# Pooling v ahead of the gather, contiguous exponentials, one second-layer job and products of zeros in a pooled-attention and mixture-of-depths kernel

## The chip, the cores and the metric

The kernel runs on one core of one Trainium2 chip. The metric is the device time of one execution in microseconds (us). Before the change its median is 304.64 us over three runs (303.97 to 305.81). The profile that is read below is of one further execution, whose span from the first to the last instruction is 305.4 us.

The core has five engines that matter here. TensorE (PE) multiplies matrices and writes to PSUM, VectorE (DVE) and ScalarE (ACT) do elementwise work, GpSimd (POOL) does elementwise work on data in SBUF and starts the indirect transfers, and SyncE (SP) starts the loads. PSUM is used here as four single banks (`bank0` to `bank3`) and two accumulators (`pA`).

## The reference

Two blocks follow each other. Attention takes q, k and v of shape (8 batches, 8 heads, 576 tokens, 64); k and v are averaged over windows of 8 tokens, so that 72 pooled keys remain. Then, for each batch, a gate picks 128 of the 576 rows, and these rows go through a two-layer network.

```python
k_p = k.reshape(B, H, Sp, pool, D).mean(axis=3)
v_p = v.reshape(B, H, Sp, pool, D).mean(axis=3)
scores = scale * np.matmul(q, k_p.transpose(0, 1, 3, 2))
attn = softmax(scores)                                # written out in the reference
x = np.matmul(attn, v_p)                              # then (B, H, S, D) -> (B, S, H*D = 512)

scores = np.einsum('bsd,d->bs', x, w_gate)
out = x.copy()
for b in range(B):
    top_idx = np.argpartition(-scores[b], capacity)[:capacity]      # capacity 128
    xe = x[b, top_idx]
    h = np.maximum(xe @ w1, 0.0)                      # w1: 512 x 1024
    ye = h @ w2                                       # w2: 1024 x 512
    g = 1.0 / (1.0 + np.exp(-scores[b, top_idx]))
    out[b, top_idx] = x[b, top_idx] + g[:, None] * ye
```

All inputs and outputs are float32.

## The kernel before

The order of the instructions is written by hand. The work is cut into 21 steps. A step computes the scores of some tokens against the pooled keys (`scores`), their exponentials, the products with the pooled v (`attend`) and the division by the sums (`norm`). Batches go in pairs: a pair (e, o) of an even and an odd batch takes five steps, two of e, one with the last tokens of both, two of o; the first pair takes six (steps 0 to 5), so that step 6 is the first of batch 2. The main loop is this; `run(u, slot)` runs the jobs that were put down for a slot of a step with `at(u, slot, ...)`:

```python
for u in range(NU + 1):
    for a, x in enumerate(chunks):
        if x[0] == u:
            attend(a)
            norm(a)
    run(u, 0)
    if u + 1 < NU:
        scores(u + 1)
    if u < NU:
        store_x(u)
    if u + 2 < NU:
        q_trans(u + 2)
    for slot in range(1, 5):
        run(u, slot)
```

Each engine works through its own instructions in this order. The jobs are: `pool_k` and `pool_v`, which sum the windows of 8 (the last of `pool_v` also multiplies by the gate's weights); `k_trans` and `gate_v` on VectorE, which finish them; `row_bcast`, `count` and `one_hot`, which rank the rows of a batch; `gather`, which fetches the picked rows; `gate`; `x_trans`, which turns them; `hidden`, a half of the first layer; `finish`, a half of the second.

```python
    def pool_v(b, g, eng):
        x = VR[b, g]
        VP[b] = vps[b % 2]
        h = slice(HG * g, HG * g + HG)
        eng.tensor_tensor(out=x[:, :, 0:4, :], in0=x[:, :, 0:4, :], in1=x[:, :, 4:8, :], op=OP.add)
        eng.tensor_tensor(out=x[:, :, 0:2, :], in0=x[:, :, 0:2, :], in1=x[:, :, 2:4, :], op=OP.add)
        eng.tensor_tensor(out=VP[b][:, h, 0:D], in0=x[:, :, 0, :], in1=x[:, :, 1, :], op=OP.add)
        nc.gpsimd.tensor_tensor(out=x[:, :, 2, :], in0=VP[b][:, h, 0:D], in1=wg[:, h, :], op=OP.mult)
    def gate_v(b, g):
        h = slice(HG * g, HG * g + HG)
        nc.vector.tensor_reduce(out=VP[b][:, h, D + 1], in_=VR[b, g][:, :, 2, :], axis=AX.X, op=OP.add)
# ... in scores(), for a step of one batch: 8 exponentials out of four banks, two of each bank
            ET[u] = [[work.tile([128, 2, C], FT, name=f"et{i}{c}") for i in range(4)] for c in range(2)]
            for c in range(2):
                for i in range(4):
                    x = p[i].rearrange("p s one (n t c g) -> p (s one n) c g t", n=2, c=2, g=G)[:, :, c]
                    y = ET[u][c][i].rearrange("p s (n g t) -> p (s n) g t", n=2, g=G)
                    if c == 0:
                        x, y = (z.rearrange("p a g t -> p a t g") for z in (x, y))
                    nc.scalar.activation(y, x, AF.Exp, scale=exp_scale)
# ... in attend(): one product for each head and half, which reads VP[b], the pooled v with its gate's column
                nc.tensor.matmul(PA[a][TL * t : TL * t + TL, g, E * n : E * n + E], e, VP[b][:, h, :], start=True, stop=True)
# ...
        p = accumulator()[:, 0, 0 : 2 * NC].rearrange("p (k c) -> p k c", k=2)
# ... (products with ones, then two operations on VectorE)
    def x_trans(b):
        p = bank([128, DB, cap])
        for d in range(DB):
            nc.tensor.transpose(p[:, d, :], XR[b][:, 128 * d : 128 * d + 128], ident[:cap, :cap])
        XG[b] = work.tile([128, DB, cap], FT, name="xg", bufs=1)
        nc.scalar.copy(out=XG[b], in_=p)
# ...
    def finish(b, part, p):
        idx, g = GV[b]
        if part == 0:
            gate_end(b)
        c = slice(DM // 2 * part, DM // 2 * part + DM // 2)
        p = p.rearrange("p a b -> p (a b)")[:cap, 0 : DM // 2]
        for f in range(FB):
            n, m = divmod(f, FB // 2)
            nc.tensor.matmul(p, HT[b, n][:, m, :], w2[:, f, c], start=(f == 0), stop=(f == FB - 1))
        nc.vector.scalar_tensor_tensor(Y[b][:, c], p, g, XR[b][:, c], op0=OP.mult, op1=OP.add)
        if part == 1:
            i = nc.gpsimd.indirect_dma_start(
                out=out_rows, out_offset=bass.IndirectOffsetOnAxis(ap=idx[:, :1], axis=0), in_=Y[b], in_offset=None)
            others(i, b, (store, scat, gath))
            scat[b] = [i]
    def dense(b, i, first=False):
        p = accumulator()[:, 0, 0 : FB // 2 * cap].rearrange("p (a b) -> p a b", b=cap) if first else bank([128, FB // 2, cap])
        (hidden, finish)[i // 2](b, i % 2, p)
```

The jobs of the first pair and of a later pair (e, o) that isn't the last, cut to what the change touches; `s` is the first step of the pair, and x and y are the two batches of the pair after:

```python
    for b, (steps_of, dense_of) in {
        0: (((2, 1), (3, 0), (3, 3), (5, 0)), ((5, 3, False), (5, 3, False), (6, 1, True), (7, 1, True))),
        1: (((5, 1), (6, 0), (6, 3), (7, 3)), ((8, 1, True), (9, 1, True), (9, 2, False), (10, 1, True))),
    }.items():
        for f, x in zip((row_bcast, one_hot, gather, x_trans), steps_of):
            at(*x, f, b)
        at(*steps_of[0], count, b)
        at(*steps_of[3], gate, b)
        for i, (u, slot, first) in enumerate(dense_of):
            at(u, slot, dense, b, i, first)
# ... for e in range(2, B, 2): s = 6 + 5 * (e // 2 - 1); o = e + 1
            at(s + 5, 3, gather, o)
            at(s + 6, 3, x_trans, o)
            at(s + 6, 3, gate, o)
            for i in range(4):
                at(s + 5 + i // 2, 1 + i % 2, dense, e, i, i % 2 == 0)
            at(s + 7, 2, dense, o, 0)
            at(s + 8, 1, dense, o, 1, True)
            at(s + 8, 2, dense, o, 2)
            at(s + 9, 2, dense, o, 3)
# ...
            at(s + 2, 4, pool_k, x, pool)
            at(s + 2, 4, pool_v, x, 0, pool)
            at(s + 3, 4, pool_v, x, 1, pool)
            at(s + 3, 4, k_trans, x)
            at(s + 4, 4, gate_v, x, 0)
            at(s + 4, 4, gate_v, x, 1)
            at(s + 4, 4, pool_k, y, pool)
            at(s + 5, 4, pool_v, y, 0, pool)
            at(s + 5, 4, k_trans, y)
            at(s + 6, 4, pool_v, y, 1, pool)
            at(s + 6, 4, gate_v, y, 0)
            at(s + 6, 4, gate_v, y, 1)
```

## Time and profile before

| What | Value |
|---|---|
| time, median of three runs | 304.64 us |
| span of the profiled execution | 305.4 us |
| PE matmul busy | 232.1 us (76%), 2922 instructions |
| PE weight load busy | 205.4 us (67%) |
| DVE busy | 139.3 us (46%) |
| POOL busy | 130.7 us (43%) |
| ACT busy | 76.9 us (25%) |
| mean granted TensorE clock | 0.903 |
| moved by DMA | 46.94 MB, mean 154 GB/s |

An engine's busy time is summed over its instructions, and "idle before" a line is the time that the engine stood still ahead of it, with the instruction that released it. Matmuls in float32 show as two records each. L-numbers are lines of the kernel: L323 is the scores, L338 the exponentials, L352 attend, L489 the first layer, L502 and L503 the second, L248 to L252 the pooling of v, L256 `gate_v`, L455 and L457 the gather's index and its start, L479 and L481 `x_trans`, L505 the scatter of the finished rows.

### The profile page before, as it was taken

The page shows a single profiled execution, that of the slowest core. Times are in us where ns is not written, and L with a number is a line of the kernel's source. Part 1 is how long each engine was busy: PE and PEld are TensorE (multiplying, and loading weights), DVE is VectorE, ACT ScalarE, POOL GpSimd, SP SyncE. Part 2 cuts the span into 40 slices and gives each one's busy share as a digit, 9 for nine tenths or more (in the row PEclk, how much of TensorE's full clock was granted, in tenths as well). Part 3 has the DMA queues.
Part 4 walks back from the last instruction along what each step waited for, and adds up shares of the span by engine and source line. Part 5 has one row for each costly group of instructions (what it writes and reads, how often), then busy time and mean ns, then how long its engine had stood idle before and what let it go on. Part 6 is the DMA issues. An engine that isn't in the chain of part 4 may idle for free.

```text
span 305.4 us, 7024 instructions
## 1 busy us (share of the span) xinstructions
PE 232.1 (76%) x2922; PEld 205.4 (67%) x2922; DVE 139.3 (46%) x416; ACT 76.9 (25%) x185; POOL 130.7 (43%) x135
## 2 busy tenths in 40 slices
PE   0488565389992979949992799789982799799990
PEld 0367455269871869839981589679972689698970
DVE  5977727450561381674331452853620631711111
ACT  9045431131310404413111224224210323100100
POOL 8589703970078910870257920753537000201101
PEclk9999977559997799977997599999997899999997
DMA  7998999935483652317733422122121002311001
GB/s 288 356 359 297 323 403 406 367 148 157 153 330 114 204 222 69 88 60 243 289 101 113 164 105 71 50 91 71 36 69 36 34 2 71 104 38 34 36 0 45
DMA packets 13528, 46.94 MB, mean 154 GB/s; under 512 B 1584, under 2 KB 1584, under 8 KB 11440
## 3 DMA queue, kind: packets, MB, share of 16 engines
q1 hardware_dynamic: 9008, 32.77, 30.0%
q10 hardware_dynamic: 3200, 9.44, 9.2%
q0 software_dynamic: 1280, 4.20, 4.2%
q8 instruction: 25, 0.41, 0.6%
q14 instruction: 15, 0.12, 0.1%
HBM read 34.87 MB, written 11.53 MB: 152 GB/s over the span
## 4 chain that ended last, share of the span: by engine, by line
PE 54%; POOL 13%; issue 11%; DVE 10%; DMA 8%; ACT 2%; ACTq 1%; POOLq 0%; DVEq 0%; SPq 0%
PE bank L502 13%; PE bank L323 11%; PE pA L489 9%; PE bank L489 8%; PE pA L352 8%; POOL vraw L248 4%; PE pA L502 4%; DMA qraw<-in_q_dram 3%; DMA xr<-out_dram,idx 2%; POOL vraw L249 2%; DMA out_dram<-xs 2%; ACT et L338 2%; DVE ge L432 1%; POOL vp L250 1%; DVE kh L236 1%
## 5 line engine op out<-in xcount | busy, mean ns | idle before, releaser
L338 ACT ACTIVATE et<-bank 128x256 f32<-128x256 f32 x128 | 49.0, 535 | 104.6 <-PE bank L323 104.6
L323 PE MATMUL bank<-qt,kt 32*128 32x256 f32 (+1 forms) x768 | 51.5, 412 | 13.9 <-DVE qt L308 12.1
L323 PEld LDWEIGHTS bank<-qt,kt 32*128 32x128 f32 x768 | 40.2, 222 | 18.7 <-POOL auxb L200 12.1
L352 PE MATMUL pA<-vp,et 128*64 128x66 f32 x1024 | 40.0, 240 | 12.9 <-DVE vp L256 7.1
L352 PEld LDWEIGHTS pA<-vp,et 128*64 128x64 f32 x1024 | 36.7, 152 | 16.5 <-DVE vp L256 6.0
L455 POOL TENSOR_SCALAR idx<-tok 128x1 int32<-128x1 f32 x8 | 1.8, 225 | 106.7 <-DVE tok L453 99.3
L502 PE MATMUL bank<-w,ht 128*128 128x256 f32 x176 | 39.7, 380 | 1.7 <-ACT et L338 1.7
L489 PE MATMUL bank<-xg,w 128*128 128x128 f32 x288 | 35.3, 284 | 4.5 <-ACT et L338 3.8
L489 PEld LDWEIGHTS bank<-xg,w 128*128 128x128 f32 x288 | 34.2, 199 | 5.7 <-ACT et L338 4.8
L502 PEld LDWEIGHTS bank<-w,ht 128*128 128x128 f32 x176 | 32.9, 190 | 6.1 <-ACT et L338 1.9
L248 POOL TENSOR_TENSOR vraw<-vraw 128x1024 f32<-128x1024 f32 x14 | 33.0, 2355 | 0.3
L489 PEld LDWEIGHTS pA<-xg,w 128*128 128x128 f32 x224 | 25.5, 192 | 3.0 <-issue 2.0
L489 PE MATMUL pA<-xg,w 128*128 128x128 f32 x224 | 26.9, 278 | 0.7 <-ACT xg L481 0.7
L503 DVE SCALAR_TENSOR_TENSOR y<-bank,g,xr 128x256 f32<-128x256 f32 x11 | 5.3, 484 | 48.3 <-PE bank L502 48.3
L505 POOL DMA_INDIRECT out_dram<-y,idx x8 | 9.1, 1142 | 41.6 <-DVE y L503 25.6
L432 DVE SCALAR_TENSOR_TENSOR ge<-pA,sc,before 128x128 bf16<-128x128 f32 (+3 forms) x40 | 18.4, 506 | 12.8 <-PE pA L416 12.8
L352 PE MATMUL pA<-vp,el 128*64 128x66 f32 x128 | 8.8, 260 | 19.5 <-DVE vp L256 18.7
L308 DVE STREAM_TRANSPOSE qt<-qraw 128x1024 f32<-128x1024 f32 (+1 forms) x24 | 23.0, 968 | 0.1
L368 DVE TENSOR_TENSOR xs<-pA,rzall 128x512 f32<-128x512 f32 x32 | 22.1, 691 | 1.1
L352 PEld LDWEIGHTS pA<-vp,el 128*64 128x64 f32 x128 | 7.1, 165 | 21.1 <-DVE vp L256 19.7
L360 DVE RECIPROCAL rzall<-pA 128x8 f32<-128x8 f32 (+1 forms) x37 | 7.6, 205 | 27.2 <-PE pA L352 27.2
L502 PE MATMUL pA<-w,ht 128*128 128x256 f32 x80 | 18.6, 386 | 0.0
(91 smaller groups left out, 249.2 us busy)
## 6 DMA issues: line engine op xcount, KB each, us to landing
kraw<-in_k_dram SPq DMA_DIRECT2D x8, 1152.0 KB, 15.9
qraw<-in_q_dram SPq DMA_DIRECT2D x8, 1152.0 KB, 7.5
vraw<-in_v_dram SPq DMA_DIRECT2D x16, 512.0 KB, 4.3
out_dram<-xs ACTq DMA_DIRECT2D x32, 256.0 KB, 4.1
w<-in_moe_w_dram SPq DMA_DIRECT2D x2, 2048.0 KB
vraw<-in_v_dram SPq DMA_DIRECT2D x16, 64.0 KB
out_dram<-xh ACTq DMA_DIRECT2D x8, 128.0 KB, 4.3
wg<-in_moe_w_gate_dram SPq DMA_DIRECT2D x1, 256.0 KB, 7.6
```

Of the source, the lines that this page charges most:

```text
L248: eng.tensor_tensor(out=x[:, :, 0:4, :], in0=x[:, :, 0:4, :], in1=x[:, :, 4:8, :], op=OP.add)
L249: eng.tensor_tensor(out=x[:, :, 0:2, :], in0=x[:, :, 0:2, :], in1=x[:, :, 2:4, :], op=OP.add)
L308: nc.vector.transpose(out=QT[u][:, :, n : n + x.shape[1], :].rearrange("p j t c -> p t j c"), in_=x)
L323: nc.tensor.matmul(p[i][:, s, n, :], KT[x][r, j, s, :], QT[u][r, j, t, G * s : G * s + G], start=(j == 0), stop=(j == 1))
L338: nc.scalar.activation(y, x, AF.Exp, scale=exp_scale)
L352: nc.tensor.matmul(PA[a][TL * t : TL * t + TL, g, E * n : E * n + E], e, VP[b][:, h, :], start=True, stop=True)
L360: nc.vector.reciprocal(rz, o[:, :, :, D])
L368: nc.vector.tensor_tensor(out=y[r, i, :].rearrange("p (g n d) -> p g n d", g=2, d=D), in0=o[:, :, :, 0:D], in1=rz.rearrange("p g (n one) - ...
L432: nc.vector.scalar_tensor_tensor(x, y, s, m, op0=OP.is_ge, op1=OP.mult, accum_out=k[:, c, 0:1])
L489: nc.tensor.matmul(p[:, n, :], w1[:, d, 128 * f : 128 * f + 128], XG[b][:, d, :], start=(d == 0), stop=(d == DB - 1))
L502: nc.tensor.matmul(p, HT[b, n][:, m, :], w2[:, f, c], start=(f == 0), stop=(f == FB - 1))
L505: i = nc.gpsimd.indirect_dma_start(out=out_rows, out_offset=bass.IndirectOffsetOnAxis(ap=idx[:, :1], axis=0), in_=Y[b], in_offset=None)
```

## The change

Five things change.

1. Where v is pooled. For every odd batch but the first, both halves of `pool_v` are now put down ahead of the neighbouring gather, in slot 0 of the step, so that GpSimd does them before it turns to the gather and to the scatter after it. For batch 2 the first half moves ahead of the first gather. For batch 0 one product moves from GpSimd to VectorE.
2. The exponentials. Half of them were read and written in a permuted order; all are now written contiguously. From step 6 on they go bank by bank, so that a bank is free after two of them.
3. The second layer. It is done as one job of 8 products of 512 columns rather than two jobs of 8 products of 256 columns, for all batches but batch 1, and its place is that of one of the two.
4. The jobs of the first two batches are put down anew, one by one: among others the ranking of batch 0 comes after `attend` of step 3, the first `x_trans` after the scores of step 6, and a half of the first layer of batch 1 moves from step 8 to step 7. The copy of batch 0's turned rows goes to VectorE, and the ranking of batch 0 uses a single bank.
5. TensorE multiplies zeros in bf16, 36 products of 512 columns while it waits for the first keys, and 11 after the scores of step 0. Their result isn't used. They are for the TensorE clock.

The diff:

```diff
@@ -111,6 +111,16 @@
         QR[b] = work.tile([128, TG, D], FT, name="qraw")
         nc.sync.dma_start(out=QR[b], in_=q[b].rearrange("h (g t) d -> (h g) t d", g=G))
 
+
+    zeros = const.tile([128, 512], BF)
+    nc.vector.memset(zeros, 0.0)
+
+    def keep_busy(n):
+        p = psum.tile([C, 2, 512], FT, name="pA")
+        for _ in range(n):
+            nc.tensor.matmul(p[:, 0, :], zeros[:, 0:C], zeros, start=True, stop=True)
+
+    keep_busy(36)
     vraws = [const.tile([128, HG, POOLW, D], FT, name=f"vraw{i}") for i in range(4)]
     nc.vector.memset(vraws[0], 0.0)
 
@@ -241,7 +251,7 @@
         nc.vector.tensor_reduce(out=y[:, :, 0:128:2], in_=x[:, :, 0:64, :], axis=AX.X, op=OP.add)
         nc.vector.tensor_reduce(out=y[:, :, 1:128:16], in_=x[:, :, 64:SP, :], axis=AX.X, op=OP.add)
 
-    def pool_v(b, g, eng):
+    def pool_v(b, g, eng, mult=nc.gpsimd):
         x = VR[b, g]
         VP[b] = vps[b % 2]
         h = slice(HG * g, HG * g + HG)
@@ -249,7 +259,7 @@
         eng.tensor_tensor(out=x[:, :, 0:2, :], in0=x[:, :, 0:2, :], in1=x[:, :, 2:4, :], op=OP.add)
         eng.tensor_tensor(out=VP[b][:, h, 0:D], in0=x[:, :, 0, :], in1=x[:, :, 1, :], op=OP.add)
 
-        nc.gpsimd.tensor_tensor(out=x[:, :, 2, :], in0=VP[b][:, h, 0:D], in1=wg[:, h, :], op=OP.mult)
+        mult.tensor_tensor(out=x[:, :, 2, :], in0=VP[b][:, h, 0:D], in1=wg[:, h, :], op=OP.mult)
 
     def gate_v(b, g):
         h = slice(HG * g, HG * g + HG)
@@ -329,13 +339,11 @@
                                      p[i].rearrange("p s n (t g) -> p (s n) g t", t=QT4), AF.Exp, scale=exp_scale)
         else:
             ET[u] = [[work.tile([128, 2, C], FT, name=f"et{i}{c}") for i in range(4)] for c in range(2)]
-            for c in range(2):
-                for i in range(4):
-                    x = p[i].rearrange("p s one (n t c g) -> p (s one n) c g t", n=2, c=2, g=G)[:, :, c]
-                    y = ET[u][c][i].rearrange("p s (n g t) -> p (s n) g t", n=2, g=G)
-                    if c == 0:
-                        x, y = (z.rearrange("p a g t -> p a t g") for z in (x, y))
-                    nc.scalar.activation(y, x, AF.Exp, scale=exp_scale)
+
+            for c, i in [(c, i) for c in range(2) for i in range(4)] if u < 6 else [(c, i) for i in range(4) for c in range(2)]:
+                nc.scalar.activation(
+                    ET[u][c][i].rearrange("p s (n g t) -> p (s n) g t", n=2, g=G),
+                    p[i].rearrange("p s one (n t c g) -> p (s one n) c g t", n=2, c=2, g=G)[:, :, c], AF.Exp, scale=exp_scale)
 
     def attend(a):
         u, x = chunks[a]
@@ -434,7 +442,7 @@
 
     def one_hot(b):
 
-        p = accumulator()[:, 0, 0 : 2 * NC].rearrange("p (k c) -> p k c", k=2)
+        p = (accumulator()[:, 0, 0 : 2 * NC] if b else bank([C, 2 * NC])).rearrange("p (k c) -> p k c", k=2)
         for c in range(NC):
             for i in range(c, NC):
                 nc.tensor.matmul(p[:, 0, c : c + 1], GE[b][i][:, c, :], ones, start=(i == c), stop=(i == NC - 1))
@@ -478,7 +486,10 @@
         for d in range(DB):
             nc.tensor.transpose(p[:, d, :], XR[b][:, 128 * d : 128 * d + 128], ident[:cap, :cap])
         XG[b] = work.tile([128, DB, cap], FT, name="xg", bufs=1)
-        nc.scalar.copy(out=XG[b], in_=p)
+        if b == 0:
+            nc.vector.tensor_copy(out=XG[b], in_=p)
+        else:
+            nc.scalar.copy(out=XG[b], in_=p)
 
     def hidden(b, part, p):
 
@@ -490,27 +501,30 @@
                                  start=(d == 0), stop=(d == DB - 1))
         nc.scalar.activation(HT[b, part], p[:, 0 : FB // 2, :], AF.Relu)
 
-    def finish(b, part, p):
+    def finish(b, part, parts, p):
 
         idx, g = GV[b]
         if part == 0:
             gate_end(b)
-        c = slice(DM // 2 * part, DM // 2 * part + DM // 2)
-        p = p.rearrange("p a b -> p (a b)")[:cap, 0 : DM // 2]
+        c = slice(DM // parts * part, DM // parts * (part + 1))
+        p = p.rearrange("p a b -> p (a b)")[:cap, 0 : DM // parts]
         for f in range(FB):
             n, m = divmod(f, FB // 2)
             nc.tensor.matmul(p, HT[b, n][:, m, :], w2[:, f, c], start=(f == 0), stop=(f == FB - 1))
         nc.vector.scalar_tensor_tensor(Y[b][:, c], p, g, XR[b][:, c], op0=OP.mult, op1=OP.add)
-        if part == 1:
+        if part == parts - 1:
             i = nc.gpsimd.indirect_dma_start(
                 out=out_rows, out_offset=bass.IndirectOffsetOnAxis(ap=idx[:, :1], axis=0), in_=Y[b], in_offset=None)
             others(i, b, (store, scat, gath))
             scat[b] = [i]
 
-    def dense(b, i, first=False):
-
-        p = accumulator()[:, 0, 0 : FB // 2 * cap].rearrange("p (a b) -> p a b", b=cap) if first else bank([128, FB // 2, cap])
-        (hidden, finish)[i // 2](b, i % 2, p)
+    def dense(f, b, part, first=False, parts=1):
+
+        p = accumulator()[:, 0, :].rearrange("p (a b) -> p a b", b=128) if first else bank([128, 4, 128])
+        if f is hidden:
+            hidden(b, part, p[:, :, 0:cap])
+        else:
+            finish(b, part, parts, p)
 
 
 
@@ -521,16 +535,25 @@
 
 
     pool = nc.gpsimd
-    for b, (steps_of, dense_of) in {
-        0: (((2, 1), (3, 0), (3, 3), (5, 0)), ((5, 3, False), (5, 3, False), (6, 1, True), (7, 1, True))),
-        1: (((5, 1), (6, 0), (6, 3), (7, 3)), ((8, 1, True), (9, 1, True), (9, 2, False), (10, 1, True))),
-    }.items():
-        for f, x in zip((row_bcast, one_hot, gather, x_trans), steps_of):
-            at(*x, f, b)
-        at(*steps_of[0], count, b)
-        at(*steps_of[3], gate, b)
-        for i, (u, slot, first) in enumerate(dense_of):
-            at(u, slot, dense, b, i, first)
+    at(3, 0, row_bcast, 0)
+    at(3, 0, count, 0)
+    at(3, 1, one_hot, 0)
+    at(3, 1, gather, 0)
+    at(5, 1, x_trans, 0)
+    at(5, 2, gate, 0)
+    at(5, 2, row_bcast, 1)
+    at(5, 2, dense, hidden, 0, 0)
+    at(5, 2, count, 1)
+    at(5, 3, dense, hidden, 0, 1)
+    at(6, 0, one_hot, 1)
+    at(6, 1, dense, finish, 0, 0, True)
+    at(6, 3, gather, 1)
+    at(7, 1, x_trans, 1)
+    at(7, 2, gate, 1)
+    at(7, 2, dense, hidden, 1, 0)
+    at(8, 2, dense, hidden, 1, 1)
+    at(9, 1, dense, finish, 1, 0, True, 2)
+    at(10, 2, dense, finish, 1, 1, False, 2)
     for e in range(2, B, 2):
         s = 6 + 5 * (e // 2 - 1)
         o, last = e + 1, e + 2 == B
@@ -542,24 +565,21 @@
         at(s + 4, 3, x_trans, e)
         at(s + 4, 3, gate, e)
         if last:
-            for i, f in enumerate((one_hot, gather, None, x_trans)):
-                at(s + 5, 1, dense, e, i, i == 0)
-                if f:
-                    at(s + 5, 1, f, o)
-            at(s + 5, 1, gate, o)
-            for i in range(4):
-                at(s + 5, 1, dense, o, i)
+            for f, *x in ((dense, hidden, e, 0, True), (one_hot, o), (dense, hidden, e, 1), (gather, o),
+                          (dense, finish, e, 0), (x_trans, o), (gate, o), (dense, hidden, o, 0), (dense, hidden, o, 1),
+                          (dense, finish, o, 0)):
+                at(s + 5, 1, f, *x)
         else:
             at(s + 5, 0, one_hot, o)
             at(s + 5, 3, gather, o)
             at(s + 6, 3, x_trans, o)
             at(s + 6, 3, gate, o)
-            for i in range(4):
-                at(s + 5 + i // 2, 1 + i % 2, dense, e, i, i % 2 == 0)
-            at(s + 7, 2, dense, o, 0)
-            at(s + 8, 1, dense, o, 1, True)
-            at(s + 8, 2, dense, o, 2)
-            at(s + 9, 2, dense, o, 3)
+            at(s + 5, 1, dense, hidden, e, 0, True)
+            at(s + 5, 2, dense, hidden, e, 1)
+            at(s + 6, 1, dense, finish, e, 0, True)
+            at(s + 7, 2, dense, hidden, o, 0)
+            at(s + 8, 1, dense, hidden, o, 1, True)
+            at(s + 9, 2, dense, finish, o, 0)
 
             x, y = e + 2, e + 3
             at(s, 1, load_k, x)
@@ -577,9 +597,9 @@
             at(s + 4, 4, gate_v, x, 0)
             at(s + 4, 4, gate_v, x, 1)
             at(s + 4, 4, pool_k, y, pool)
-            at(s + 5, 4, pool_v, y, 0, pool)
+            at(s + 5, 0, pool_v, y, 0, pool)
+            at(s + 5, 0, pool_v, y, 1, pool)
             at(s + 5, 4, k_trans, y)
-            at(s + 6, 4, pool_v, y, 1, pool)
             at(s + 6, 4, gate_v, y, 0)
             at(s + 6, 4, gate_v, y, 1)
 
@@ -594,21 +614,21 @@
     at(0, 2, load_w2)
     at(0, 2, k_trans, 1)
     at(0, 2, load_k, 3)
-    at(2, 0, gate_v, 1, 0)
-    at(2, 0, gate_v, 1, 1)
+    at(2, 1, gate_v, 1, 0)
+    at(2, 1, gate_v, 1, 1)
     at(2, 1, load_v, 3, 0)
     at(2, 1, load_v, 3, 1)
     at(2, 2, pool_k, 2, pool)
+    at(3, 0, pool_v, 2, 0, pool)
     at(3, 2, load_q, 3)
-    at(3, 4, pool_v, 2, 0, pool)
+    at(3, 4, pool_v, 2, 1, pool)
     at(4, 1, k_trans, 2)
-    at(4, 1, pool_v, 2, 1, pool)
     at(5, 4, gate_v, 2, 0)
     at(5, 4, gate_v, 2, 1)
     at(5, 4, pool_k, 3, pool)
-    at(6, 4, pool_v, 3, 0, pool)
+    at(6, 0, pool_v, 3, 0, pool)
+    at(6, 0, pool_v, 3, 1, pool)
     at(6, 4, k_trans, 3)
-    at(7, 1, pool_v, 3, 1, pool)
     at(7, 4, gate_v, 3, 0)
     at(7, 4, gate_v, 3, 1)
 
@@ -626,8 +646,9 @@
     k_trans(0)
     q_trans(0)
     scores(0)
+    keep_busy(11)
     pool_v(0, 0, nc.vector)
-    pool_v(0, 1, nc.vector)
+    pool_v(0, 1, nc.vector, nc.vector)
     load_k(2)
     gate_v(0, 0)
     gate_v(0, 1)
```

## The prediction

> **What bounds the kernel now.** I read the page's slices first, then TensorE's waits, then its timeline beside GpSimd's.
>
> The slices say that no engine bounds the whole span. TensorE (PE) is near full from the ninth slice (61 us) on, but for dents; before that its share swings, and its clock falls to five tenths in the eighth and ninth slice (53 to 69 us).
>
> ```profile
> PE   0488565389992979949992799789982799799990
> PEclk9999977559997799977997599999997899999997
> DMA  7998999935483652317733422122121002311001
> ```
>
> DMA is full or nearly so in the first eight slices (to 61 us) and loose after them. So there are two regimes: up to 60 us the loads and the first gather set the pace, later TensorE's own work plus what it waits for. The list of its waits (total, number, longest in us):
>
> ```profile
> PE pA L352 <- DVE vp L256: 25.8, 8, 5.9
> PE bank L323 <- DVE qt L308: 12.1, 1, 12.1
> PE bank L479 <- DMA xr<-out_dram,idx: 8.0, 2, 7.2
> PE pA L352 <- DVE ge L432: 4.7, 2, 2.9
> PE bank L489 <- ACT et L338: 3.8, 3, 1.6
> PE bank L451 <- ACT et L338: 2.3, 1, 2.3
> PE bank L502 <- ACT et L338: 1.7, 1, 1.7
> ```
>
> The first row is the largest that isn't the start-up. Its releaser is a short VectorE reduction; who held that one is seen on GpSimd's timeline (start, length; idle before in brackets):
>
> ```profile
> 216.46 0.22 POOL L455 TENSOR_SCALAR idx<-tok 128x1 int32<-128x1 f32 x1 [7.82 <-DVE tok L453]
> 217.33 1.07 POOL L457 DMA_INDIRECT xr<-out_dram,idx  x1 [0.65 <-POOL idx L455]
> 218.43 2.36 POOL L248 TENSOR_TENSOR vraw<-vraw 128x1024 f32<-128x1024 f32 x1
> ...
> 228.33 1.23 POOL L505 DMA_INDIRECT out_dram<-y,idx  x1 [4.63 <-DVE y L503]
> 229.59 2.35 POOL L248 TENSOR_TENSOR vraw<-vraw 128x1024 f32<-128x1024 f32 x1
> ```
>
> GpSimd stands idle 7.82 us with batch 7's v in SBUF, because the gather of batch 5 heads its queue, and again 4.63 us for the scatter of batch 4. The second half of v then ends at 234.84, while TensorE stands before it:
>
> ```profile
> 227.90 0.33 PE L352 MATMUL pA<-vp,el 128*64 128x66 f32 x2
> 229.05 0.69 PE L352 MATMUL pA<-vp,el 128*64 128x66 f32 x16 [0.82 <-DVE vp L256]
> 235.34 1.14 PE L352 MATMUL pA<-vp,el 128*64 128x66 f32 x14 [5.61 <-DVE vp L256]
> 236.42 3.52 PE L323 MATMUL bank<-qt,kt 32*128 32x256 f32 x32
> ...
> 242.21 1.05 PE L489 MATMUL bank<-xg,w 128*128 128x128 f32 x7 [1.59 <-ACT et L338]
> ```
>
> The scores after the wait take 3.52 us; at full clock the same 32 records take 2.01 (at 182.48). So a wait costs more than its length. In the early stretch TensorE waits 7.17 us for the first gather and then works at half clock:
>
> ```profile
> 57.83 1.09 PE L479 MATMUL bank<-ident,xr 128*128 128x128 f32 x4 [7.17 <-DMA xr<-out_dram,idx]
> 59.59 3.79 PE L323 MATMUL bank<-qt,kt 32*128 32x256 f32 x32 [0.68 <-ACT xg L481]
> 63.31 1.33 PE L416 MATMUL pA<-ident,sc 128*128 128x128 f32 x5
> 65.74 8.88 PE L489 MATMUL bank<-xg,w 128*128 128x128 f32 x64 [1.09 <-ACT et L338]
> ```
>
> [...] the first scores (12.14) and the first attend (17.44) take 3.80 us each, twice the 2.01 and 2.1 of later, full rate comes at 21.2, and half rate returns after the waits of 5.6 to 7.2 us. [...] Here the permuted exponentials write floats 16 bytes apart; in the first set (15.92, 16.34, 16.80, 17.26) they start 0.46 apart, the contiguous ones 0.26 to 0.3.
>
> **The change part by part.** "Gain" is against the trace before.
>
> *v of batches 3, 5 and 7.* One half costs GpSimd 5.3 us (218.43 to 223.71). Pooling of k for batch 7 ends at 208.64; both halves then fill 208.65 to about 219.2. The gather of batch 5, ready at 216.46, starts some 2.7 later; its landing (3.5 us median after issue) comes near 224, before TensorE asks for it at 227.37. So nothing is given back, and waits of 5.88 (at 99.38), 5.60 (168.82) and 5.61 (235.34) go. What is left is VectorE's own chain after the second layer: L503, now 512 wide, say 0.75 (as L432 of 512), the gate 0.69, one reduction 0.42, less 0.6 of transposes: 1.2 rather than 0.82. Sum 17.1 - 3 x 0.4 = 15.9. The scores after them return to full rate: 3.23 + 3.80 + 3.52 - 3 x 2.01 = 4.5.
>
> *Exponentials.* Bank 0 was free after the fifth one, about 2.2 us after the scores; now after two, about 0.65, which the row broadcast (0.76) covers. The waits of 1.11, 1.67 and 1.59 (175.98, 198.74, 242.21) go: 4.4. The fourth of 1.09 (65.74) is counted below.
>
> *Start.* [...] Scores and attend are warm, but attend still waits for v, now with one product more on VectorE: it starts at 17.85, not 17.44, and ends near 20.0, not 21.24. Gain 1.2.
>
> *First gather and step 6.* Batch 0's ranking no longer holds an accumulator in step 3 (the 2.92 us wait) and starts right after attend. From 20.0 on: scores and attend of steps 1 to 3 end near 32.6 (GpSimd's v of batch 1 ends at 30.5, not 32.3, as one product left it), the ranking's 3.1 us on VectorE near 36.8, the gather's index products near 38.9 rather than 44.5. GpSimd meanwhile pools k of batch 2 (30.5 to 34.6) and half of its v (to 39.8), so the index follows at 40. Before, 5.79 us of unexplained waiting lay between index and gather start; I keep it, so start near 46 (50.85 before) and, at 6.9 us to landing, x near 52.8 (57.7 before). Step 6's scores, which used to come after, now go into this hole: their q lands at 44.3 or a little sooner, the transposes of q and k follow, scores from about 47 to 51. After landing only the transposes, a copy and no 3.79 us of scores lie ahead of the first layer: it starts near 54.5 to 55.5, not 65.74. Gain 10 to 11 in all here, with the 1.2 of the start and the 1.09 inside it.
>
> *Steps 7 to 10.* The second layer of batch 0 (7 us in one piece, the same columns) now comes before batch 1's gather, whose start waits also for the scatter (1.2): about 3.1 us after the layer ends, landing 4 to 7 later. TensorE has attend 2.1 and scores 2.3 to do meanwhile, so it waits 2 to 5, say 3.3, plus 0.7 for the copy: a loss of 3.1 against the 0.87 before. The wait of 1.81 for the ranking of batch 2 (111.10) goes, as a half layer now lies between: gain 1.8. The 4.47 at 135.64 came because the ranking of batch 3 was broadcast only after a second-layer job (130.03); it now stands ahead: 1.1 is left, and attend takes 2.1 rather than 3.79: 5.1.
>
> *One job in the second layer.* 16 records of 256 columns take 3.47 us, two jobs 6.92 in the tail: the columns set that, so halving the number of products brings nothing. The last L503 is 0.27 longer: -0.3.
>
> Sum: 15.9 + 4.5 + 4.4 + 10.5 - 3.1 + 1.8 + 5.1 - 0.3 = 38.8, so 304.6 - 38.8 = 265.8.
>
> **Rivals.** (1) *The wait only changes its name.* With v early, the gather sits behind 10.6 us of pooling, and TensorE waits at L479 instead. For it: in-order GpSimd, and the small slack at batch 3 (pooling of v of batch 5 may end about 2.5 us after its index is ready). Against: 7 us of second layer lie between. Were it true for all three, some 10 us less: 276. (2) *DMA is the bound up to 63 us.* The DMA row is full there; if q of batch 2 and the gather land as before, the early gain is about 6 (only the scores move behind the wait): 270. If also batch 3's loads bind, 275. (3) *Zeros don't open the gate, or there are too many.* [...] (4) *All waits were hiding work:* once PE is dense its 205 us of weight loads or GpSimd's 131 us would show. Against: a pair of batches has 55.3 us of PE busy in 66.5 us (170 to 236.5), and GpSimd 31.5.
>
> **Range and chances.** All my corrections for what I can't see go one way: new waits and half-clock stretches eat gains, and few things add to them, but for the unexplained 5.79 us. I say 267 us. 258 if that wait goes too and batch 1's gather is quick; 279 if rivals 1 and 2 both hold in part. To be within 2% of 304.6 five sixths of the sum would have to fail; chances 0.96, 0.03 and 0.01.
>
> **What would show it.** Right: the row of L352 waiting for L256 falls from 25.8 to 5 or less; GpSimd shows L248 to L252 twice in a row ahead of L457 for batches 3, 5, 7; the first scores take about 2.0; the first layer starts near 55; a pair takes 57 us; the exponentials start 0.28 apart. Wrong: L479 waiting for the gather with over 8 us in total beyond the first, the first scores later than 12.5, or the first layer of batch 0 after 60.

## The result and the profile after

The changed kernel takes 263.9 us, the median of four runs (261.77 to 265.45), against 305.23 (303.97 to 306.6) for the kernel before in the same session: a ratio of 0.8641, with a 95% interval of 0.8561 to 0.872. Predicted were 267 us. The profiled execution has a span of 261.2 us and a mean granted clock of 0.972 (0.903 before). In the kernel after, L333 is the scores, L344 the exponentials, L360 attend, L424 the row broadcast, L500 the first layer, L513 the second, L516 the scatter, L258 to L262 the pooling of v, L266 `gate_v`, L463 and L465 the gather's index and its start, L487 `x_trans`, L121 the products of zeros. Experiments with a line more or less shift these by a few.

The page's slices of the kernel after (one is 6.5 us, against 7.6 before):

```profile
PE   8757885689995999989998999899989999898970
PEclk9997999999995999999999999999999999999996
DMA  7999799999984584249734823112212042111001
```

The clock is whole but for the fourth, the thirteenth and the last slice; the deep dents of the second half are gone. DMA is now near full for eleven slices, to 72 us: the loads are as many, and work that hurries ahead runs into them. Where that shows first is GpSimd, which waits 6.55 us for k of batch 3 (to 57.87).

TensorE's waits, in the kernel after (total, number, longest in us):

```profile
PE pA L360 <- DVE vp L266: 10.0, 6, 4.7
PE bank L333 <- DVE kt L252: 3.0, 3, 2.3
PE bank L487 <- DMA xr<-out_dram,idx: 2.7, 1, 2.7
...
PE bank L487 <- ACT et L344: 0.8, 1, 0.8
```

The first row was 25.8, with a longest of 5.9. Of the 10.0 that are left, 4.73 lie in the start. Of the rows in which the layers waited for exponentials, the one of 3.8 is down to a single wait of 0.28 and the one of 1.7 is gone. The first row misses the "5 or less" that the prediction named as a sign of being right, because of the start; without it 5.3 would be left. GpSimd's timeline of the kernel after, where batch 7's v stands next to batch 5's gather as in the prediction's lines, shows why the first row fell:

```profile
174.72 2.36 POOL L258 TENSOR_TENSOR vraw<-vraw 128x1024 f32<-128x1024 f32 x1
...
179.95 2.36 POOL L258 TENSOR_TENSOR vraw<-vraw 128x1024 f32<-128x1024 f32 x1
...
184.56 0.69 POOL L262 TENSOR_TENSOR vraw<-vp,wg 128x256 f32<-128x256 f32 x1
185.33 0.21 POOL L463 TENSOR_SCALAR idx<-tok 128x1 int32<-128x1 f32 x1
185.82 1.08 POOL L465 DMA_INDIRECT xr<-out_dram,idx  x1 [0.28 <-POOL idx L463]
194.40 1.20 POOL L516 DMA_INDIRECT out_dram<-y,idx  x1 [7.49 <-DVE y L514]
```

Both halves of v run back to back into what was idle time; the idle time now stands ahead of the scatter, where nobody waits. On TensorE's timeline of the kernel after, the same place:

```profile
193.16 0.60 PE L487 MATMUL bank<-ident,xr 128*128 128x128 f32 x4
193.69 0.33 PE L360 MATMUL pA<-vp,el 128*64 128x66 f32 x2
195.11 1.15 PE L360 MATMUL pA<-vp,el 128*64 128x66 f32 x30 [1.09 <-DVE vp L266]
196.19 2.01 PE L333 MATMUL bank<-qt,kt 32*128 32x256 f32 x32
```

`x_trans` doesn't wait for the gather, one wait of 1.09 is left for v, and the scores take 2.01 us, at a granted clock of 1.00. The early stretch, with the second gather:

```profile
43.43 2.09 PE L360 MATMUL pA<-vp,et 128*64 128x66 f32 x64
...
50.33 2.01 PE L333 MATMUL bank<-qt,kt 32*128 32x256 f32 x32 [2.26 <-DVE kt L252]
53.10 0.66 PE L487 MATMUL bank<-ident,xr 128*128 128x128 f32 x4 [0.76 <-ACT et L344]
...
54.58 7.38 PE L500 MATMUL bank<-xg,w 128*128 128x128 f32 x64 [0.28 <-ACT et L344]
...
80.47 1.08 PE L487 MATMUL bank<-ident,xr 128*128 128x128 f32 x4 [2.69 <-DMA xr<-out_dram,idx]
82.23 5.60 PE L500 MATMUL bank<-xg,w 128*128 128x128 f32 x32 [0.68 <-ACT xg L492]
```

The first gather costs no wait any more, and step 6's scores lie ahead of `x_trans`. The first layer of batch 0 starts at 54.58 (65.74 before). Batch 1's gather is now waited for, and the half layer after that wait takes 5.60 rather than 3.84 us, with a granted clock of 0.50 from 79.12 to 85.95. And the start:

```profile
1.18 9.34 PE L121 MATMUL pA<-zeros 128*128 128x512 bf16 x36 [1.18 <-DVE zeros L116]
12.16 2.01 PE L333 MATMUL bank<-qt,kt 32*128 32x256 f32 x32 [1.64 <-DVE qt L318]
...
21.38 3.54 PE L360 MATMUL pA<-vp,et 128*64 128x66 f32 x64 [4.73 <-DVE vp L266]
```

With the zeros ahead of them the first scores take 2.01 us (3.80 before), yet attend came 4 us later than before and was slow again (3.54 us; the granted clock was 0.50 from 21.10 to 24.51). What held it is on VectorE's timeline of the kernel after (the pooling of batch 0's v):

```profile
13.88 0.43 DVE L260 TENSOR_TENSOR vp<-vraw 128x256 f32<-128x256 f32 x1
...
16.56 2.81 DVE L260 TENSOR_TENSOR vp<-vraw 128x256 f32<-128x256 f32 x1
19.41 1.50 DVE L262 TENSOR_TENSOR vraw<-vp,wg 128x256 f32<-128x256 f32 x1
```

The same addition took 0.43 us in the first half and 2.81 in the second. GpSimd's timeline of the kernel after shows its neighbour:

```profile
16.48 2.61 POOL L240 TENSOR_TENSOR kraw<-kraw 128x1152 f32<-128x1152 f32 x1 [0.51 <-DMA kraw<-in_k_dram]
```

GpSimd, which no longer has the product, had begun on k of batch 1 0.08 us before; VectorE's addition ended 0.28 us after GpSimd's operation. The product after it went the same way: its 1.50 us end at 20.91, 0.28 us after GpSimd's next operation (19.17 to 20.63). What joins the two engines here isn't shown; that GpSimd's operation makes the 2.81, a1 below shows.

Where the gain arose, from the starts of the same work in both traces. The predicted column adds up the terms of the prediction that lie ahead of each point:

| Point | before | after | gain so far | predicted |
|---|---|---|---|---|
| first layer of batch 0 starts | 65.74 | 54.58 | 11.2 | 10.5 |
| attend after the 4.47 us wait ends | 139.43 | 116.76 | 22.7 | 21.0 |
| scores after the wait for v of batch 5 start | 169.89 | 141.01 | 28.9 | 26.2 |
| those after the wait for v of batch 7 start | 236.42 | 196.19 | 40.2 | 36.0 |
| end of the span | 305.4 | 261.2 | 44.2 | 38.8 |

The two profiled executions took 307.21 and 262.99 us. The medians, 305.23 and 263.9, are 41.3 us apart, so 2.9 of the 44.2 us belong to the choice of these two executions.

### The profile page after: what moved, and what is told of

Read it like the earlier page. It is cut to its first block, busy times and chain, and to the rows that moved or that the text cites. A ratio compares the mean times of both kernels' runs of the same rounds, so it can differ in the third digit from the quotient of the medians.

```text
span 261.2 us, 6888 instructions
## 1 busy us (share of the span) xinstructions
PE 225.4 (86%) x2857; PEld 175.9 (67%) x2857; DVE 140.5 (54%) x412; ACT 64.5 (25%) x184; POOL 130.4 (50%) x134
## 4 chain that ended last, share of the span: by engine, by line
PE 67%; DVE 14%; DMA 8%; issue 4%; ACT 2%; POOL 2%; ACTq 0%; DVEq 0%; POOLq 0%
PE bank L500 15%; PE bank L513 12%; PE bank L333 12%; PE pA L513 10%; PE pA L360 9%; PE pA L500 7%; DMA qraw<-in_q_dram 5%; DMA out_dram<-xh 2%; DVE xs L376 2%; DVE kh L246 2%; PE pA L448 1%; ACT et L344 1%; DVE vp L260 1%; DVE y L475 1%; DMA out_dram<-xs 1%
## 5 line engine op out<-in xcount | busy, mean ns | idle before, releaser
L344 ACT ACTIVATE et<-bank 128x256 f32<-128x256 f32 x128 | 37.1, 411 | 73.4 <-PE bank L333 73.4
L500 PE MATMUL bank<-xg,w 128*128 128x128 f32 x352 | 43.2, 284 | 1.9 <-ACT xg L492 1.4
L333 PE MATMUL bank<-qt,kt 32*128 32x256 f32 (+1 forms) x768 | 40.7, 349 | 4.6 <-DVE kt L252 3.0
L500 PEld LDWEIGHTS bank<-xg,w 128*128 128x128 f32 x352 | 41.8, 199 | 3.4 <-ACT xg L492 2.0
L360 PE MATMUL pA<-vp,et 128*64 128x66 f32 x1024 | 35.3, 229 | 8.3 <-DVE vp L266 7.9
L360 PEld LDWEIGHTS pA<-vp,et 128*64 128x64 f32 x1024 | 33.2, 142 | 10.6 <-issue 5.2
L333 PEld LDWEIGHTS bank<-qt,kt 32*128 32x128 f32 x768 | 32.6, 185 | 7.5 <-issue 2.5
L516 POOL DMA_INDIRECT out_dram<-y,idx x8 | 9.2, 1155 | 54.6 <-DVE y L514 38.0
L258 POOL TENSOR_TENSOR vraw<-vraw 128x1024 f32<-128x1024 f32 x14 | 33.7, 2407 | 0.1
L513 PE MATMUL bank<-w,ht 128*128 128x512 f32 (+1 forms) x80 | 32.0, 553 | 0.2
L463 POOL TENSOR_SCALAR idx<-tok 128x1 int32<-128x1 f32 x8 | 1.8, 225 | 47.9 <-DVE tok L461 40.4
L513 PE MATMUL pA<-w,ht 128*128 128x512 f32 (+1 forms) x64 | 25.1, 545 | 0.0
L513 PEld LDWEIGHTS bank<-w,ht 128*128 128x128 f32 x80 | 14.8, 191 | 14.4 <-issue 13.4
L240 POOL TENSOR_TENSOR kraw<-kraw 128x1152 f32<-128x1152 f32 x7 | 18.4, 2632 | 7.2 <-DMA kraw<-in_k_dram 7.1
L500 PE MATMUL pA<-xg,w 128*128 128x128 f32 x160 | 19.2, 278 | 0.7 <-ACT xg L492 0.7
L500 PEld LDWEIGHTS pA<-xg,w 128*128 128x128 f32 x160 | 18.2, 192 | 2.3 <-issue 1.3
L513 PEld LDWEIGHTS pA<-w,ht 128*128 128x128 f32 x64 | 11.8, 190 | 11.2 <-issue 10.7
```

The source lines that it names most:

```text
L333: nc.tensor.matmul(p[i][:, s, n, :], KT[x][r, j, s, :], QT[u][r, j, t, G * s : G * s + G], start=(j == 0), stop=(j == 1))
L344: nc.scalar.activation(ET[u][c][i].rearrange("p s (n g t) -> p (s n) g t", n=2, g=G), p[i].rearrange("p s one (n t c g) -> p (s one n) c g ...
L500: nc.tensor.matmul(p[:, n, :], w1[:, d, 128 * f : 128 * f + 128], XG[b][:, d, :], start=(d == 0), stop=(d == DB - 1))
L516: i = nc.gpsimd.indirect_dma_start(out=out_rows, out_offset=bass.IndirectOffsetOnAxis(ap=idx[:, :1], axis=0), in_=Y[b], in_offset=None)
```

## The experiments

"Worth" is a difference of two ratios, times 305.2 us. A ratio is known to about 0.004 to 0.008, so differences below some 2.5 us aren't settled by themselves. The profiles of a2, a6, a8 and a11 are of executions a per cent or two slower than the fastest of their kernels (a11's took 263.7 us, where five of eight took 259.6 to 260.1), so single rows of them are used, and whole stretches only with that in mind.

### a1: the product back on GpSimd

```diff
-    pool_v(0, 1, nc.vector, nc.vector)
+    pool_v(0, 1, nc.vector)
```

> The changed kernel, but the gate's product of the second half of batch 0's v is back on GpSimd. My theory: in the changed kernel VectorE's last sum of v (2.81 us against 0.43 before) and the product after it (1.50) were held by GpSimd's sums over k of batch 1, which could start 1.3 us earlier because the product no longer stood ahead of them in GpSimd's queue[...]. Then here the sum takes 0.43 again, GpSimd starts on k only after it, attend of step 0 starts near 17.5 rather than 21.4 us, and since first stores and the loads behind them follow from it, the time falls by about 3 us, to 261. Rival: the sum was slowed by traffic of the loads into the same memory. Then it stays above 2 us here and the time stays at 264. Second rival: the start is hidden behind the loads: the sum is short again, but the time doesn't change.

Measured: 263.73 us, ratio 0.8627 (0.8569 to 0.8684): no difference from the kernel after. VectorE's timeline of a1:

```profile
16.56 0.42 DVE L260 TENSOR_TENSOR vp<-vraw 128x256 f32<-128x256 f32 x1
```

and GpSimd's:

```profile
17.12 0.68 POOL L262 TENSOR_TENSOR vraw<-vp,wg 128x256 f32<-128x256 f32 x1 [1.14 <-DVE vp L260]
17.76 2.63 POOL L240 TENSOR_TENSOR kraw<-kraw 128x1152 f32<-128x1152 f32 x1
```

The addition has the same start and the same loads beside it; only GpSimd's large operation comes after it, and it takes 0.42 us. So the 2.81 come from GpSimd, and not from DMA traffic. Attend starts at 17.46 (predicted 17.85), and the scores after it at 19.96, 4.9 us ahead of the kernel after. Nothing of this lead arrives, and TensorE's timeline of a1 shows where most of it goes:

```profile
30.93 0.69 PE L360 MATMUL pA<-vp,et 128*64 128x66 f32 x16 [0.70 <-DVE vp L266]
32.98 2.91 PE L360 MATMUL pA<-vp,et 128*64 128x66 f32 x48 [1.37 <-DVE vp L266]
```

GpSimd, which has the product back, begins on k of batch 1 at 17.76 rather than 16.48 and then works without a pause until 41.7, so that batch 1's v is finished at 32.38 rather than 31.31. The attend of step 3 starts early, at 30.93, but its second part waits 1.37 us for this v and then runs slowly (2.91 us, where a8 took 1.63), which costs 2.8 us of the lead; by 36.75 it is 1.2 us. The rest goes at reduced clock: the attend behind the first gather's index products takes 3.03 us (2.09 in the kernel after) and step 6's scores 3.48 (2.01), with a granted clock of 0.91 up to 55 us (0.97), so that the first layer starts at 55.29, 0.7 us later than in the kernel after. None of these waits is for a load.

### a2 and a5: no products of zeros

a2 is the kernel after without both calls of `keep_busy`; a5 is a1 without them.

```diff
-    keep_busy(36)
-    keep_busy(11)
```

> The changed kernel without the two runs of products of zeros. My theory: scores of step 0 take 3.8 us rather than 2.01, but attend waits for v until 21.4 us anyway, so only attend itself loses 0.3 (3.8 against 3.54): the time stays within 1 us of 263.9. Rival: the clock of the whole first stretch rests on them; then the time rises by 3 to 5 us.

> The changed kernel with the gate's product of batch 0 back on GpSimd and without the products of zeros. If the zeros pay only when attend of step 0 isn't held up, they show here: scores of step 0 end 1.9 us later, attend starts at 17.5 but takes 3.8 rather than about 2.2 us, so the time is 1.5 to 2.5 us above that of the kernel with the product on GpSimd and with zeros. Rival: the loads set the pace in this stretch, and no difference shows (within 0.7 us).

Measured: a2 267.34 us, ratio 0.8739 (0.8681 to 0.8798), 3.0 us over the kernel after; a5 265.9 us, ratio 0.8646 (0.861 to 0.8683), 0.6 us over a1. The intervals overlap in both pairs, so the medians put the zeros at 3.0 and at 0.6 us, and neither is settled. My expectations, at most 1 for a2 and 1.5 to 2.5 for a5, aren't borne out by the medians; the rival of a5, no difference beyond 0.7, fits its own. What they do is plain. TensorE's timeline of a5:

```profile
12.13 3.56 PE L332 MATMUL bank<-qt,kt 32*128 32x256 f32 x32 [12.13 <-DVE qt L317]
...
53.42 8.73 PE L499 MATMUL bank<-xg,w 128*128 128x128 f32 x64
```

Without zeros the first scores take 3.56 us (2.01 with them). But a5 still reaches the first layer at 53.42, before a1 with 55.29; then the layer takes 8.73 us (7.38). What the zeros bring early is not what is seen at the end.

### a3 and b1: v of the odd batches

a3 is the kernel after with the old places of odd v; b1 the kernel before with the new ones and nothing else.

```diff
-            at(s + 5, 0, pool_v, y, 0, pool)
-            at(s + 5, 0, pool_v, y, 1, pool)
+            at(s + 5, 4, pool_v, y, 0, pool)
             at(s + 5, 4, k_trans, y)
+            at(s + 6, 4, pool_v, y, 1, pool)
```

(a3; b1 is the reverse, and batch 3's two lines likewise.)

> The changed kernel, but v of batches 3, 5 and 7 is pooled where it was before: first half after the neighbour's gather, second half after the scatter. By the prediction's terms (15.9 us of waits and 4.5 us of slow scores) the time rises by 20 us, to 284, and three waits of 5 to 6 us for the gate's column come back. Rival: in the new order of the rest, GpSimd has the slack to take v after the gather, and the waits are short: less than 8 us more.

> The kernel before with one part of the change alone: v of batches 3, 5 and 7 pooled ahead of the gather. If the part stands by itself the time falls by 20 us, to 285, and the three waits of 5 to 6 us go. Rival: without the rest of the change the gather or the ranking takes the place of the wait, and less than 12 us are gained.

Measured: a3 282.93 us, ratio 0.926 (0.9204 to 0.9317), so undoing it costs 18.9 us; b1 282.04 us, ratio 0.9178 (0.9137 to 0.922), so alone it brings 25.1, against 20.4 in the prediction's terms. TensorE's timeline of a3:

```profile
207.89 0.69 PE L360 MATMUL pA<-vp,el 128*64 128x66 f32 x16 [1.09 <-DVE vp L266]
214.18 1.14 PE L360 MATMUL pA<-vp,el 128*64 128x66 f32 x14 [5.60 <-DVE vp L266]
215.25 3.80 PE L333 MATMUL bank<-qt,kt 32*128 32x256 f32 x32
```

The old wait is back, with slow scores behind it. A pair of batches takes 63.15 us (144.74 to 207.89), against 55.17 in the kernel after (139.94 to 195.11). The 8.0 us are 5.6 of wait, 1.7 of scores at less than full clock, and 0.7 of attend, broken in two and its second part slow (0.69 + 1.14 against 1.15). Two pairs give 16.0. At batch 3 only 0.25 us of wait came back (92.59), not 5.88. In b1, where only v was moved, 0.47 of that wait is left: the move is enough by itself to remove it there, and so are the other changes without it. The 6.2 us between b1's gain and a3's loss are about this one wait.

### a4, a9 and a10: the exponentials, whole and in parts

a4 has them as before; a9 keeps the contiguous writes and takes the old order of banks; a10 keeps the new order and writes one half 16 bytes apart.

```diff
 # a9
-            for c, i in [(c, i) for c in range(2) for i in range(4)] if u < 6 else [(c, i) for i in range(4) for c in range(2)]:
+            for c, i in [(c, i) for c in range(2) for i in range(4)]:
 # a10, and with a9's line a4
+                    if c == 0:
+                        x, y = (z.rearrange("p a g t -> p a t g") for z in (x, y))
```

> The changed kernel with the exponentials as before: half of them permuted, and the order over the banks as before in all steps. By the prediction's term the three waits of 1.1 to 1.7 us for a bank come back (4.4 us), and attend of steps 1 to 3 loses up to 0.7 each: 268 to 270. Rival: the new order of the dense jobs leaves enough between scores and the first bank's next use; then less than 2 us more.

> The changed kernel with contiguous exponentials, but always in the order of before: four banks for one half, then four for the other. Splits the 13.5 us that both halves of that part were worth together. If the order of banks counts, bank 0 is free after five exponentials of 0.28 us, so about 1.5 us after the scores rather than 0.65, and the five waits of 1.6 to 1.7 us before the layers come back as 0.5 to 0.8 each: 3 to 4 us in all, 267 to 268 us. If only the stride of the writes counts, nothing comes back: 263 to 265 us.

> The changed kernel with one half of the exponentials written 16 bytes apart as before, but in the new order of banks. If the order counts, bank 0 is free after two exponentials (0.46 and 0.28 us), and the five late waits stay away; what comes back is the early stretch, where both kernels go half by half (sets 0 to 5), and 0.7 us of ScalarE per set that the attends wait for only where they follow at once: 264 to 268 us. If the stride is the larger part, the whole 13.5 us come back less the 3 to 4 of the order: 272 to 275 us.

Measured: a4 277.45 us, ratio 0.9069 (0.8989 to 0.9149), worth 13.1 us; a9 270.29 us, 0.8821 (0.8787 to 0.8855), worth 5.5; a10 267.63 us, 0.8742 (0.8696 to 0.8788), worth 3.1. TensorE's timeline of a4, where jobs of a layer follow the scores:

```profile
154.86 3.84 PE L503 MATMUL bank<-xg,w 128*128 128x128 f32 x32 [1.61 <-ACT et L349]
173.88 7.13 PE L516 MATMUL bank<-w,ht 128*128 128x512 f32 x16 [1.68 <-ACT et L349]
```

the same two of a9:

```profile
148.81 3.84 PE L500 MATMUL bank<-xg,w 128*128 128x128 f32 x32 [0.87 <-ACT et L344]
167.08 7.13 PE L513 MATMUL bank<-w,ht 128*128 128x512 f32 x16 [0.93 <-ACT et L344]
```

and of a10:

```profile
147.26 3.84 PE L502 MATMUL bank<-xg,w 128*128 128x128 f32 x32 [0.24 <-ACT et L348]
164.89 7.13 PE L515 MATMUL bank<-w,ht 128*128 128x512 f32 x16 [0.29 <-ACT et L348]
```

Each kernel has five such places. With both old ways a job waits 1.6 to 1.7 us for a bank, with the old order alone 0.9, with the old stride alone 0.2 to 0.3, and in the kernel after not long enough to be listed. The order decides how many exponentials stand before the freed bank (five or two), and the stride how long four of these five take (in a4 those with it start 0.43 to 0.45 us apart, at 210.91; in the kernel after, without it, 0.27, at 174.93): so together they cost more than the sum of each (8.2 us against 4.5 + 1.3). Of a4's 13.1 us these five places explain 8.2. The rest is early (the first of the five at 99.86 less its wait of 1.64, against 91.64): `x_trans`, which now comes right after step 6's scores, waits 2.28 us for a bank in a4 (0.76 in the kernel after), and the first layer starts at 59.47 rather than 54.58. A part of this is the stride: the first gather's index products start at 45.55 and 45.38 in a4 and a10, which write with it, and at 43.03 and 43.22 in a9 and the kernel after, which don't, 2.2 to 2.5 us apart. How much of the rest is the early clock (see the last section) isn't told apart by single traces. a10 met its expectation, though its 3.1 us aren't settled by themselves (its interval overlaps that of the kernel after). a9, with 5.5 us by its ratio where 3 to 4 were expected, did not (the kernel before took 306.67 us in its session, so the 270.29 overstates the miss), though its five waits are only just above the 0.5 to 0.8 foreseen: in its trace another 2.6 us are lost ahead of them (the first of these jobs at 95.14 less its wait of 0.93, against 91.64).

### a6: the first pair's jobs as before

The ranking, gather and layers of batches 0 and 1, v of batch 2 and the copy of xg go back to their old places; the rest stays new.

```diff
-    at(3, 0, row_bcast, 0)
-    at(3, 1, gather, 0)
-    at(5, 1, x_trans, 0)
+    at(2, 1, row_bcast, 0)
+    at(3, 3, gather, 0)
+    at(5, 0, x_trans, 0)
 # cut: the other jobs of batches 0 and 1, v of batch 2
```

> The changed kernel, but the jobs of batches 0 and 1, and the first two halves of v of batch 2, are in their slots of before (the second layer of both in two jobs). By the prediction's terms for the first gather with step 6 (about 9 without the start) and for steps 7 to 10 (5.1 + 1.8 - 3.1) the time rises by 12 to 13 us, to 276. The unexplained wait of 5.8 us between the index and the start of the first gather should come back if it belongs to this order. Rival: the early stretch is set by the loads; then less than 6 us more.

Measured: 271.19 us, ratio 0.8815 (0.878 to 0.885), so these jobs are worth 5.3 us, and not 12 to 13; the rival, less than 6, is met. One row of GpSimd's timeline of a6 says what did not come back:

```profile
47.14 1.23 POOL L465 DMA_INDIRECT xr<-out_dram,idx  x1 [0.74 <-POOL idx L463]
```

In the kernel before, 5.79 us lay between index and gather; here, with the same jobs in the same places, 0.74. So the loss of this stall isn't owed to the moved jobs, and its 5.05 us are most of what is missing between 5.3 and 12 to 13. Also, the 5.88 us wait at batch 3 stays away, as v is early in a6 too. `x_trans` waits 5.10 us for the gather (7.17 before), and the 4.46 us wait of attend is back (123.82).

### a7: the second layer in two jobs

```diff
-            at(s + 6, 1, dense, finish, e, 0, True)
+            at(s + 6, 1, dense, finish, e, 0, True, 2)
+            at(s + 6, 1, dense, finish, e, 1, False, 2)
 # likewise for batch 0, the odd batches and the last pair
```

> The changed kernel with each second layer in two jobs of 256 columns, one right after the other, in the place of the one job. The prediction: the columns set the time, so it stays within 0.7 us of 263.9. Rival: twice the products and weight loads cost something each; at 0.1 us for each of 56 added products, 5 us more.

Measured: 263.35 us, ratio 0.8584 (0.855 to 0.8619): no difference from the kernel after.

### a8 and a11: batch 1's gather ahead of batch 0's second layer

After the wait of 2.69 us above, the obvious trial. a11 is the kernel after with this alone; a8 has a1's product too.

```diff
+    at(6, 1, gather, 1)
     at(6, 1, dense, finish, 0, 0, True)
-    at(6, 3, gather, 1)
```

> The changed kernel with the gate's product of batch 0 back on GpSimd, and the gather of batch 1 issued ahead of the second layer of batch 0 rather than behind it. Theory: the wait of 2.2 to 2.7 us for that gather goes, since some 7 us of second layer then lie between its issue and its use, and the first layer of batch 1 that was cold after it (5.60 us against 3.84) comes back to full rate: 3 to 4.5 us, so 259.5 to 261 us. Rival: TensorE must now make the gather's index products ahead of the second layer, and these wait for the one-hot rows on VectorE and then hold GpSimd ahead of v of batch 3; a wait of 1 to 3 us takes the place of the one removed: 262.5 to 265 us.

> The changed kernel, with nothing but the gather of batch 1 issued ahead of the second layer of batch 0 (the gate's product of batch 0 stays on VectorE). It tells whether the 0.846 of the run before, against 0.863 without the earlier gather, came from the gather. Theory: the wait of 2.69 us for that gather goes, the index products wait some 0.8 us for a bank in its place, and the first layer of batch 1 is no longer cold: 259 to 261 us. Rival: what is saved there is waited for later, or the layer stays cold because the half clock comes from the slack around it: 262.5 to 264.5 us.

Measured: a8 259.58 us, ratio 0.846 (0.8418 to 0.8501), 5.1 us under a1; a11 260.05 us, ratio 0.8519 (0.8486 to 0.8552), 3.7 us under the kernel after. Both intervals lie clear of those they are compared with, so this beats both kernels; whether the product on GpSimd adds to it isn't settled (the intervals of a8 and a11 overlap). TensorE's timeline of a11:

```profile
82.63 0.66 PE L487 MATMUL bank<-ident,xr 128*128 128x128 f32 x4 [0.45 <-ACT el L338]
84.67 3.84 PE L500 MATMUL bank<-xg,w 128*128 128x128 f32 x32 [1.38 <-ACT xg L492]
...
92.32 3.84 PE L500 MATMUL bank<-xg,w 128*128 128x128 f32 x32
```

The wait for the gather is gone and the half layer after it takes 3.84 us; the granted clock is 1.00 from 75 to 95 us (0.83 in the kernel after, where it was 0.50 from 79.12 to 85.95). From batch 0's first layer (58.12) to the second half of batch 1's (92.32) a11 takes 34.2 us, the kernel after 37.1 (54.58 to 91.64). In a8's trace the wait is gone as well, but that half layer still takes 6.58 us, with a granted clock of 0.83 from 75 to 95, and the stretch 37.2, so there the saving isn't visible; the timed runs of both kernels show it.

## Why the prediction was right, and where not

The sum of the terms was 265.8 us, measured were 263.9: the main lines hold, but that the number is so close is luck in part. The exponentials were counted 8.7 us too low (4.4, measured 13.1) and the jobs of the first pair some 7.5 us too high (12.8 in the prediction's terms, measured 5.3), and these errors cancel.

*v of batches 3, 5 and 7* (15.9 and 4.5 of clock). Shown: 18.9 us by undoing it, 25.1 alone. The gather that starts later gave nothing back, so rival 1 falls: no `x_trans` of batches 2 to 7 waits for a gather. Per pair 8.0 us go, against 5.2 of wait and 1.5 to 1.8 of scores predicted; missing was that the second part of attend is slow as well. At batch 3 the gain belongs to two parts, each of which removes the wait.

*Exponentials* (4.4). The mechanism was right, the size not: 13.1 us (some 10 to 17 by the intervals). I counted three waits of the old trace. In the new order five jobs of the layers stand right behind scores, and `x_trans` behind those of step 6; each would have waited 1.6 to 2.3 us. A part that removes a wait must be weighed in the order that the other parts make.

*Start* (1.2). Wrong in its step "it starts at 17.85": I priced one more product on VectorE, not what GpSimd would do with the time it was given. It started sooner on a large operation (16.48; 17.74 before), and VectorE's addition took 2.4 us longer beside it and the product some 1 us longer (an estimate from the 0.42 of an addition of the same size alone). The first scores took the 2.01 us foreseen; that products of zeros would do this was my estimate, which no trace of the kernel before shows. a1 shows that the error cost nothing in the end: with the start repaired, the time is the same, as the lead is lost again behind GpSimd and at reduced clock. Rival 3 falls: the zeros end at 10.52, the first scores start at 12.16 and take 2.01 us.

*First gather and step 6* (10 to 11). The first layer's start was met (54.5 to 55.5; 54.58), its parts not, so that it was met is luck in part. The index came at 43.79 rather than 40, and the 5.79 us of stall that I kept were 0.74: 3.8 us too early and 5.05 too late nearly cancel. The late start explains only a part of the late index, for a1 and a8 with the start repaired have it at 42.63 and 41.64. a6 puts the jobs themselves at 5.3 us. The stall's absence isn't theirs; the stall appears in both kernels built on the old text (before, and b1 with 5.75), and in none of the others that I profiled. What it is stays open.

*Steps 7 to 10.* Right in the rows: a wait of 2.69 and a copy of 0.68 against 3.3 and 0.7; 1.81 gone; 4.47 now 1.08 (predicted 1.1), with attend at 2.09. Not in the sum were 1.8 us of slow layer (5.60 against 3.84): I had counted no slow clock behind this wait (see the last section).

*One job* (-0.3). a7: no difference.

*Range.* I moved from 265.8 to 267 because what I can't see costs. Rival 2, that the loads bound the early stretch, isn't borne out: DMA is near full to 72 us, but the first layer came as early as I had said, and a1's lead is lost to GpSimd and to the clock. Rival 4 falls: the pair takes 55.2 us (57 predicted), and TensorE is busy for 52.0 of them (55.3 of 66.5 before, partly at half clock), GpSimd for 33.2, so TensorE is now the bound there.

## What to carry to other kernels

When one wait is traced to an engine's queue, as v behind the gather here (GpSimd idle for 7.82 us ahead of it in the kernel before), moving the work ahead pays the wait and the slow clock behind it (5.6 and 1.7 us of a3's 8.0 for a pair), and this could be added up from the trace. The gains of several parts can't be read one by one from the old trace: the new order creates waits that another part then removes (the exponentials), and two parts may remove the same one (batch 3). And a lead gained early is worth only what reaches the end: taking work off GpSimd let its next large operation come sooner, beside which VectorE's addition took 2.81 us rather than 0.42, giving it back made v of batch 1 later, and neither changed the time. The wait for the second gather, past all that, was worth 3.7 us.

## What was unexpected in the hardware

Products of zeros bring TensorE to full rate. In the kernel after, the first seven of the 36 start 0.40 to 0.43 us apart, those from 4.1 us on 0.22 apart, and the first scores behind them take 2.01 us, against 3.56 in a5, 3.79 in a2 and 3.80 in the kernel before, all three without zeros. The granted clock doesn't show this: over the first scores it reads 1.00 in the kernel before and in the kernel after.

Where the clock falls varies from run to run. The kernel after, a3, a7, a9 and a11 have the same instructions on TensorE up to the attend behind the first gather's index products. It took 2.09 us in the kernel after and in a9, but 3.79 in a3, a7 and a11. TensorE's timeline of a7:

```profile
43.49 3.79 PE L360 MATMUL pA<-vp,et 128*64 128x66 f32 x64
...
56.40 7.38 PE L500 MATMUL bank<-xg,w 128*128 128x128 f32 x64 [0.28 <-ACT et L344]
```

In the kernel after the granted clock was 0.50 from 21.10 to 24.51 us and 1.00 from there to 79.12, so over this attend too; over the first 55 us it was 0.97 there and 0.83 in a11. Why it fell in some of these runs and not in others isn't shown.

The clock also fell behind a shorter wait than those behind which the prediction counted half clock (4.47 to 7.17 us). In the kernel after it was 0.50 from 79.12 to 85.95 us, over the half layer of 5.60 us. TensorE had stood still since 77.78, so for 1.34 us when it fell, in a wait of 2.69.

The first layer started at 54.58, 56.40 and 58.12 us in the kernel after, a7 and a11, but the second half of batch 1's at 91.64, 92.22 and 92.32 (in a11 with its gather moved, which saves a wait between the two). Single traces of this early stretch can't be compared to better than 3.5 us, and most of such a difference was made up later.
